# A gated linear recurrence with a SoLU feed-forward on one core: the constants' load moves behind the first inputs, and every step gets a new place in a written order

## The chip, the cores and the metric

The kernel runs on one core of a Trainium2 chip. The metric is device time in microseconds (us): the median over several executions of the whole program. A profile of one execution, with the times of all instructions, semaphores and DMA packets, stands beside the times.

## The reference

All arrays are float32. There are 4 batches, 8 heads, 768 positions, head dimension 48; the feed-forward has width 1024 over 3072 tokens of 384. The weights come as float64 and are converted on the chip.

```python
mag = np.sqrt(a_re * a_re + a_im * a_im)
scale = np.minimum(mag, 0.999) / (mag + 1e-06)
a_re_n, a_im_n = (a_re * scale, a_im * scale)
for t in range(S):                       # S_re, S_im start at zero, (B, H, D, D)
    ar, ai = (a_re_n[:, :, t, :, None], a_im_n[:, :, t, :, None])
    new_re = ar * S_re - ai * S_im
    new_im = ar * S_im + ai * S_re
    kv = np.einsum('bhd,bhe->bhde', k[:, :, t], v[:, :, t])
    S_re, S_im = (new_re + kv, new_im)
    y[:, :, t] = np.einsum('bhd,bhde->bhe', q[:, :, t], S_re)
# y is laid out as (B*S, H*D) = x, then:
h = x @ w_in
e = np.exp(h - np.max(h, axis=-1, keepdims=True))
solu = h * e / (np.sum(e, axis=-1, keepdims=True) + 1e-09)
ln = (solu - mean(solu)) / np.sqrt(var(solu) + 1e-06) * g_ln
out = ln @ w_out
```

## The kernel before

The 3072 tokens are cut into 24 chunks of 128 (6 stretches of time by 4 batches); two neighbouring chunks make a group, so there are 12 groups. The recurrence is done chunk by chunk in closed form: the logarithm of the gate's size and its angle are summed along time with matmuls against a triangle, q and k are scaled and turned by them, and then a chunk is causal attention plus a carried state of 96 by 48 per head. Behind it the same chunk goes through the feed-forward.

The work is written as small named steps, `name:number`, with a group's number or a chunk's. Those that matter here:

- Loads of a group, each one DMA on SP's queue: `load_ar`, `load_ai`, `load_q`, `load_k`, `load_v` (384 KB), `load_vr` (four DMAs of 48 KB). Group 0's a_re and a_im come in two halves of 192 KB, `load_ara`, `load_arb`, `load_aia`, `load_aib` (line 706), one for each chunk.
- Preparation of a group: `inverse` (two ACT passes, lines 824 and 825), `ratio` (two DVE passes, 830 and 831), `sure`, `tangent`, `square`, `secant`, `fourth`, `size` (852), `eps`, `lnm` (859), then the matmuls `total0`, `total1` (f_L), their exponentials `grow` and `decay`, `trig` (a table load on ACT, line 986), `angle` (922), `on` (927), from group 3 on a split in a high and a low part, `xh` (864) and `xl` (871), the matmuls `phase0`, `phase1`, and `nearest`, `part`, `sin`, `cos`, `exp` (the table load back, 989). `qs` and `ks` scale q and k. Group 0 does `inverse` to `lnm` and `angle`, `sin`, `cos` in halves, with an a or b at the end of the name.
- A chunk's attention: `q2`, `k2` and `kqb` (a block transpose on DVE, 1009) with `kqt0` (four DMAs), or for chunks 0 and 1 `qt`, `kt` (transposes on PE, 1021) with `qT`, `kT` (copies on ACT, 1027); `score0`, `score1` (1054), `mask0` (1059), `values` (1087), `carry`, `add`.
- A chunk's feed-forward: `turned_x` (1121), `up0`, `up1` (1128), `exp0`, `solu0` (1140), `spread`, `blocks` (1158) with `away` (four DMAs), or `zt` with `zT`; `down0`, `down1` (1193), `scale`, `store`.
- The weights, in seven pieces: `fetch` (DMA), `raised` (ACT, 752), `convert` (three DVE passes, 758 to 762); then `mean`, `meansum`, `centre` fold the mean and g_ln into w_out. `again` and `inspect` read each piece a second time for a check of its range; `judge` to `flag` make one word of all checks, which decides at the end whether a slower general path runs.

Each engine works through its instructions in the order in which the steps stand in one written string, `ORDER`; a step waits only for its own operands and buffers. A place in `ORDER` is therefore a place in five queues at once. The constants `f_mats` (identity, triangle and others, 320 KB, line 1280) are the only input that is loaded from ACT's queue, and stand ahead of all steps:

```python
    to_exp()
    nc.scalar.dma_start(out=mats, in_=nc.inline_tensor(fast_constants(), ...)...)
    ...
    for s in ORDER.split():
        nm, i = s.split(":")
        go(nm, int(i))
```

Two PSUM buffers (`ps_t`) serve `total`, `phase`, `qt`, `kt` and `zt` in turn; `f_bits`, which `raised` writes, has one buffer and shares it with `blocks`.

Of the kernel before, what the change touches and what calls it, by code (L numbers as in the profile page):

```python
# [516 lines left out]
init:0 load_aia:0 load_ara:0 inversea:0 load_arb:0 ratioa:0 load_aib:0 surea:0 load_q:0 tangenta:0 fetch:5 fetch:1  # L517
inverseb:0 squarea:0 ratiob:0 secanta:0 sureb:0 sizea:0 load_v:0 tangentb:0 epsa:0 load_k:0 lnma:0 squareb:0 secantb:0
fourthb:0 sizeb:0 total0:0 epsb:0 fourtha:0 raised:5 lnmb:0 decay0:0 grow0:0 total1:0 grow1:0 decay1:0 fetch:0 trig:0
anglea:0 convert:5 phase0:0 last:0 raised:1 qs0:0 angleb:0 convert:1 phase1:0 nearest0:0 part0:0 turn_ends:0  # L520
nearest1:0 ks0:0 ks1:0 sina:0 cosa:0 load_ai:1 qs1:0 part1:0 q2:0 tot:0 sinb:0 k2:0 cosb:0 exp:0 qt1:0 load_ar:1 qT1:0
raised:0 q2:1 kt1:0 k2:1 convert:0 kT1:0 inverse:1 ratio:1 kt0:0 qt0:0 qT0:0 kT0:0 fetch:2 score1:0 fetch:6 qt0:1
qT0:1 load_vr:0 score0:0 qt1:1 sure:1 raised:2 load_q:1 mask0:0 values:0 tangent:1 kt1:1 fetch:3 square:1 secant:1
turned_x:0 convert:2 qT1:1 up0:0 fetch:4 raised:6 size:1 eps:1 convert:6 lnm:1 fourth:1 onward:0 up1:0 gain:0 total1:1
load_k:1 kT1:1 raised:3 exp0:0 grow1:1 total0:1 decay0:1 grow0:1 carry:1 convert:3 solu0:0 decay1:1 trig:1 angle:1
kt0:1 phase1:1 ks1:1 qs0:1 kT0:1 add:1 phase0:1 ks0:1 score1:1 raised:4 nearest0:1 score0:1 nearest1:1 convert:4
part0:1 carry:0 part1:1 mean:0 mean:3 mean:7 add:0 sin:1 cos:1 mask0:1 load_q:2 q2:2 k2:2 mean:1 zt0:0 exp:1 load_ar:2
mean:4 mean:2 inverse:2 values:1 mean:5 kqb:2 turned_x:1 load_ai:2 ratio:2 mean:6 zT0:0 meansum:0 again:5 last:1
centre:3 centre:7 up1:1 sure:2 tangent:2 load_v:1 kqt0:2 square:2 zt1:0 centre:1 centre:2 secant:2 centre:0 centre:4
size:2 centre:6 eps:2 centre:5 up0:1 k2:3 turn_ends:1 qs1:1 score1:2 lnm:2 onward:1 centred:0 load_vr:1 score0:2 tot:1  # L530
down0:0 total0:2 zT1:0 total1:2 load_k:2 q2:3 exp0:1 fourth:2 mask0:2 down1:0 solu0:1 decay0:2 grow0:2 grow1:2
load_ar:3 decay1:2 kqb:3 trig:2 mixed:1 zt0:1 kqt0:3 last:2 values:2 angle:2 spread:0 zT0:1 on:2 phase1:2 ks1:2 norm:0
qs0:2 turned_x:2 phase0:2 carry:2 load_ai:3 nearest1:2 nearest0:2 up0:2 part1:2 part0:2 sin:2 add:2 cos:2 ks0:2 k2:4
q2:4 centred:1 exp:2 zt1:1 zT1:1 inverse:3 scale:0 up1:2 kqb:4 score1:3 score0:3 down0:1 mask0:3 ratio:3 exp0:2
turn_ends:2 spread:1 sure:3 solu0:2 load_q:3 values:3 tangent:3 load_v:2 down1:1 square:3 tot:2 turned_x:3 secant:3
size:3 load_k:3 carry:3 qs1:2 up0:3 kqt0:4 eps:3 norm:1 up1:3 k2:5 onward:2 zt1:2 lnm:3 lh:3 zt0:2 exp0:3 q2:5 scale:1
zT0:2 zT1:2 fourth:3 score1:4 ll:3 score0:4 mixed:0 total0:3 load_vr:2 total1:3 down0:2 kqb:5 down1:2 solu0:3 decay0:3
grow0:3 grow1:3 decay1:3 mask0:4 add:3 centred:2 trig:3 blocks:3 values:4 angle:3 on:3 xh:3 kqt0:5 store:1 store:0
spread:2 xl:3 last:3 phase1:3 turned_x:4 phase0:3 ks0:3 ks1:3 qs0:3 nearest0:3 score1:5 load_ar:4 centred:3 score0:5
nearest1:3 carry:4 load_ai:4 norm:2 part0:3 up0:4 part1:3 sin:3 cos:3 up1:4 mask0:5 turn_ends:3 exp:3 add:4 scale:2  # L540
k2:6 q2:6 away:3 inverse:4 values:5 exp0:4 kqb:6 ratio:4 down0:3 load_q:4 solu0:4 spread:3 turned_x:5 sure:4 load_v:3
tangent:4 qs1:3 down1:3 carry:5 kqt0:6 square:4 blocks:4 secant:4 size:4 onward:3 up0:5 away:4 eps:4 k2:7 norm:3 up1:5
q2:7 lnm:4 lh:4 tot:3 fourth:4 score1:6 ll:4 score0:6 exp0:5 total0:4 load_vr:3 load_k:4 kqb:7 total1:4 kqt0:7 solu0:5
scale:3 decay0:4 grow0:4 grow1:4 decay1:4 mask0:6 add:5 down0:4 trig:4 down1:4 centred:5 values:6 angle:4 on:4 xh:4
centred:4 qs0:4 xl:4 spread:4 last:4 store:2 phase1:4 turned_x:6 phase0:4 ks1:4 nearest0:4 ks0:4 nearest1:4 blocks:5
score1:7 carry:6 load_ai:5 part0:4 load_ar:5 part1:4 norm:4 score0:7 up0:6 sin:4 add:6 turn_ends:4 cos:4 exp:4 scale:4
away:5 store:3 inverse:5 mask0:7 up1:6 k2:8 q2:8 kqb:8 values:7 spread:5 exp0:6 ratio:5 down0:5 sure:5 load_q:5
solu0:6 turned_x:7 load_v:4 tangent:5 down1:5 square:5 qs1:4 kqt0:8 blocks:6 secant:5 onward:4 carry:7 up0:7 norm:5
size:5 eps:5 q2:9 k2:9 away:6 load_vr:4 lnm:5 up1:7 load_k:5 lh:5 fourth:5 scale:5 exp0:7 score1:8 ll:5 score0:8
total0:5 tot:4 kqb:9 total1:5 down0:6 kqt0:9 solu0:7 grow1:5 decay1:5 mask0:8 decay0:5 grow0:5 trig:5 down1:6 add:7  # L550
centred:7 blocks:7 values:8 angle:5 on:5 inspect:5 xh:5 centred:6 xl:5 spread:6 phase1:5 last:5 qs0:5 store:4
turned_x:8 phase0:5 ks1:5 load_ar:6 nearest1:5 nearest0:5 ks0:5 carry:8 load_ai:6 score0:9 score1:9 part1:5 part0:5
mask0:9 up1:8 sin:5 norm:6 up0:8 cos:5 add:8 turn_ends:5 scale:6 exp:5 inverse:6 store:5 k2:10 q2:10 values:9 kqb:10
ratio:6 exp0:8 solu0:8 away:7 turned_x:9 onward:5 down0:7 load_q:6 sure:6 down1:7 load_v:5 spread:7 tangent:6 square:6
blocks:8 qs1:5 kqt0:10 carry:9 secant:6 fourth:6 up0:9 norm:7 size:6 k2:11 away:8 eps:6 lnm:6 tot:5 load_vr:5 up1:9
q2:11 lh:6 scale:7 exp0:9 load_k:6 score0:10 score1:10 ll:6 total0:6 kqb:11 total1:6 down0:8 kqt0:11 solu0:9 grow1:6
decay1:6 mask0:10 decay0:6 grow0:6 trig:6 down1:8 add:9 centred:9 blocks:9 angle:6 values:10 on:6 xh:6 centred:8
store:6 xl:6 qs0:6 spread:8 last:6 phase1:6 turned_x:10 phase0:6 nearest0:6 ks1:6 nearest1:6 score1:11 carry:10
load_ai:7 score0:11 ks0:6 load_ar:7 away:9 part0:6 part1:6 cos:6 up0:10 sin:6 norm:8 mask0:11 up1:10 turn_ends:6
scale:8 exp:6 add:10 inverse:7 spread:9 store:7 values:11 k2:12 q2:12 kqb:12 ratio:7 exp0:10 down0:9 onward:6 solu0:10  # L560
load_q:7 turned_x:11 sure:7 down1:9 tangent:7 qs1:6 carry:11 load_v:6 kqt0:12 square:7 blocks:10 up0:11 secant:7
size:7 norm:9 eps:7 k2:13 away:10 load_vr:6 scale:9 lnm:7 tot:6 up1:11 q2:13 lh:7 fourth:7 exp0:11 score1:12 load_k:7
ll:7 score0:12 total0:7 kqb:13 total1:7 down0:10 centred:10 kqt0:13 solu0:11 grow1:7 decay1:7 mask0:12 decay0:7
grow0:7 trig:7 down1:10 add:11 blocks:11 angle:7 values:12 on:7 xh:7 last:7 store:8 spread:10 centred:11 qs0:7 xl:7
ks0:7 phase1:7 turned_x:12 phase0:7 nearest1:7 ks1:7 nearest0:7 score0:13 score1:13 part1:7 part0:7 mask0:13 sin:7
load_ar:8 away:11 carry:12 load_ai:8 up0:12 cos:7 add:12 norm:10 turn_ends:7 scale:10 exp:7 store:9 up1:12 k2:14 q2:14
inverse:8 values:13 kqb:14 ratio:8 exp0:12 solu0:12 down0:11 load_q:8 turned_x:13 sure:8 down1:11 load_v:7 tangent:8
carry:13 qs1:7 spread:11 kqt0:14 square:8 blocks:12 secant:8 norm:11 size:8 onward:7 k2:15 tot:7 eps:8 away:12 lnm:8
load_vr:7 fourth:8 up0:13 lh:8 load_k:8 up1:13 q2:15 score1:14 score0:14 ll:8 scale:11 total0:8 kqb:15 total1:8
exp0:13 decay0:8 grow0:8 centred:12 mask0:14 grow1:8 decay1:8 down0:12 kqt0:15 solu0:13 trig:8 down1:12 add:13  # L570
centred:13 blocks:13 angle:8 values:14 on:8 xh:8 store:10 spread:12 xl:8 last:8 phase1:8 turned_x:14 phase0:8 ks0:8
score0:15 qs0:8 nearest0:8 score1:15 ks1:8 nearest1:8 part0:8 carry:14 load_ai:9 part1:8 sin:8 norm:12 mask0:15 cos:8
add:14 load_ar:9 up1:14 turn_ends:8 exp:8 up0:14 away:13 k2:16 q2:16 scale:12 inverse:9 store:11 values:15 kqb:16
ratio:9 exp0:14 spread:13 load_v:8 solu0:14 turned_x:15 sure:9 down0:13 load_q:9 down1:13 tangent:9 blocks:14 square:9
# [38 lines left out]
def whole(ctx, tc, flag, q, k, v, a_re, a_im, moe_w_in, moe_w_out, moe_g_ln, out):  # L613
# [663 lines left out]


    to_exp()
    nc.scalar.dma_start(out=mats, in_=nc.inline_tensor(fast_constants(), name="f_mats_np").ap().rearrange("p (n t) -> p n t", n=5))  # L1280
    nc.vector.memset(unit, 1.0)
    nc.vector.memset(quarter, -0.5 * math.pi)
    nc.vector.memset(small, math.log(1e-6))
# [90 lines left out]
```

## Time and profile before

| | before |
|---|---|
| median of 3 runs | 415.65 us (415.19 to 415.83) |
| profiled execution: time | 415.1 us |
| profiled execution: span, first to last instruction | 413.1 us |
| PE / DVE / ACT / POOL busy | 379.1 / 337.0 / 299.0 / 64.5 us |
| mean granted TensorE clock | 0.996 |
| bytes moved by DMA | 74.17 MB, mean 180 GB/s |
| first matmul | 13.27 us |

Times in the text are counted from the span's start. The time of an execution is 2.0 us over its span. PE is TensorE's matmuls, DVE VectorE, ACT ScalarE, POOL GpSimd, SP the engine that issues nearly all DMAs; PEq, SPq and so on are the engines' queues. In a timeline's row stand the start, the time taken, the engine, the source line, the operation, what it writes and reads, how many were merged (x), and in brackets the idle time of the engine before it and what ended that.

### The profile page before, as it was taken

Reading aid. Unit: us, or ns where it says so; the run is one execution under the profiler, and the core shown is the slowest. Engines: PE = TensorE matmul, PEld = TensorE weight load, DVE = VectorE, ACT = ScalarE, POOL = GpSimd, SP = SyncE. Lnnn points to the kernel's source line nnn. Section 1 sums busy time; section 2 is a strip of 40 time slices with the busy share of each in tenths; the row PEclk is TensorE's granted clock in tenths of the full one; section 3 lists DMA queues with packets and bytes.
Section 4 is the critical chain, followed back from the end, with each engine's and each line's share of the span. In section 5 each row is a group of like instructions: output and inputs, shape, how many; then the busy total and the mean of one; then the engine's idle time right before and its main releaser. Section 6 shows DMA issues by size and latency. Waiting matters only on the chain.

```text
span 413.1 us, 15874 instructions
## 1 busy us (share of the span) xinstructions
PE 379.1 (92%) x6968; PEld 202.7 (49%) x6968; DVE 337.0 (82%) x414; ACT 299.0 (72%) x487; POOL 64.5 (16%) x140
## 2 busy tenths in 40 slices
PE   0368779999999999999999999999999999999995
PEld 0025334455645554654554554555645656546543
DVE  3798999779799899898899889988988988855530
ACT  4997977977887777887877976877976967721332
POOL 3000000112112112112122112112112122101111
PEclk9999999999999999999999999999999999999998
DMA  9995947695877778877787877967759768797551
GB/s 216 286 280 153 222 101 171 159 211 128 207 165 170 167 177 180 182 157 167 179 175 165 207 163 160 206 157 172 163 138 215 158 155 206 232 208 187 171 216 49
DMA packets 167741, 74.17 MB, mean 180 GB/s; under 512 B 142576, under 2 KB 156016, under 8 KB 166896
## 3 DMA queue, kind: packets, MB, share of 16 engines
q1 hardware_dynamic: 167376, 72.64, 74.7%
q8 instruction: 57, 0.93, 0.9%
q10 hardware_dynamic: 288, 0.43, 0.4%
q14 instruction: 20, 0.16, 0.1%
HBM read 38.87 MB, written 4.72 MB: 106 GB/s over the span
## 4 chain that ended last, share of the span: by engine, by line
PE 81%; ACT 8%; DVE 5%; DMA 2%; issue 1%; SPq 1%; DVEq 0%; ACTq 0%
PE f_h L1128 28%; PE f_o L1193 27%; PE f_y L1087 9%; PE f_score L1054 7%; PE f_d L1095 3%; PE f_L L876 2%; PE f_phase L876 2%; DMA f_q<-in_q_dram 1%; DMA f_ar<-in_a_re_dram 1%; ACT f_cs L951 1%; PE f_y L1203 1%; PE f_o L1203 1%; ACT L986 1%; ACT L989 1%; DVE f_kb L1009 1%
## 5 line engine op out<-in xcount | busy, mean ns | idle before, releaser
L1128 PE MATMUL f_h<-f_w_in,f_xT 128*32 128x512 f32 x1152 | 131.4, 593 | 1.4 <-ACT f_xT L1121 1.2
L1193 PE MATMUL f_o<-f_w_mix,f_zT 128*32 128x384 f32 x1280 | 108.6, 487 | 0.0
L1128 PEld LDWEIGHTS f_h<-f_w_in,f_xT 128*32 128x32 f32 x1152 | 40.9, 110 | 66.4 <-issue 64.3
L1193 PEld LDWEIGHTS f_o<-f_w_mix,f_zT 128*32 128x32 f32 x1280 | 42.8, 110 | 54.1 <-issue 51.5
L1009 DVE STREAM_TRANSPOSE f_kb<-f_kq 128x1536 f32<-128x1536 f32 x22 | 56.5, 2570 | 1.4 <-DMA f_kqT<-f_kb 0.7
L1140 DVE SCALAR_TENSOR_TENSOR f_z<-f_h,f_z 128x1024 f32<-128x1024 f32 x24 | 29.1, 1213 | 13.5 <-ACT f_z L1136 13.5
L1180 POOL TENSOR_SCALAR f_s<-f_s,f_sum 128x1 f32<-128x1 f32 x24 | 11.7, 485 | 182.1 <-ACT f_z L1174 181.9
L1136 ACT ACTIVATE f_z<-f_h 128x1024 f32<-128x1024 f32 x24 | 24.4, 1018 | 21.0 <-PE f_h L1128 21.0
L1087 PE MATMUL f_y<-f_att,f_v 128*16 128x128 f32 (+1 forms) x384 | 36.7, 273 | 0.8 <-DVE f_att L1059 0.8
L1054 PEld LDWEIGHTS f_score<-f_kqT 96*32 96x32 f32 x1536 | 32.5, 112 | 10.0 <-issue 10.0
L1087 PE MATMUL f_y<-f_att,f_vr 128*32 128x128 f32 x384 | 36.8, 273 | 0.0
L1059 DVE TENSOR_TENSOR f_att<-f_score,f_mats 128x1024 f32<-128x1024 f32 x24 | 29.3, 1220 | 8.5 <-PE f_score L1054 8.4
L1054 PE MATMUL f_score<-f_kqT 96*32 96x64 f32 (+3 forms) x1536 | 34.0, 238 | 0.0
L1087 PE MATMUL f_y<-f_kqT,f_state 96*32 96x128 f32 (+1 forms) x640 | 33.2, 272 | 0.0
L1174 ACT ACTIVATE f_z<-f_z,f_less 128x1024 f32<-128x1024 f32 x24 | 27.3, 1138 | 0.0
L869 POOL TENSOR_TENSOR f_ll<-f_lr,f_lh 128x768 fp32r<-128x768 f32 x9 | 16.6, 1849 | 65.6 <-ACT f_lh L864 57.9
L1087 PEld LDWEIGHTS f_y<-f_att,f_v 128*32 128x32 f32 (+1 forms) x384 | 22.0, 103 | 7.5 <-issue 6.4
L1158 DVE STREAM_TRANSPOSE f_zb<-f_z 128x1024 f32<-128x1024 f32 x20 | 24.8, 1238 | 0.0
L1000 DVE TENSOR_TENSOR f_kq<-f_cs,f_k 128x768 f32<-128x768 f32 x24 | 22.9, 955 | 2.1 <-ACT f_cs L951 1.2
L1000 DVE TENSOR_TENSOR f_kq<-f_cs,f_q 128x768 f32<-128x768 f32 x24 | 22.9, 953 | 1.1 <-PE f_d L1095 0.5
L1087 PEld LDWEIGHTS f_y<-f_att,f_vr 128*32 128x32 f32 x384 | 22.3, 109 | 1.7 <-issue 1.7
L1171 POOL TENSOR_SCALAR f_less<-f_sum 128x1 f32<-128x1 f32 x24 | 6.3, 266 | 88.7 <-DVE f_z L1140 88.7
(124 smaller groups left out, 643.9 us busy)
## 6 DMA issues: line engine op xcount, KB each, us to landing
f_kqT<-f_kb SPq DMA_DIRECT2D x88, 192.0 KB, 3.3
f_zT<-f_zb SPq DMA_DIRECT2D x80, 128.0 KB, 3.1
f_raw<-in_moe_w_out_dram SPq DMA_DIRECT2D x14, 384.0 KB, 5.0
f_raw<-in_moe_w_in_dram SPq DMA_DIRECT2D x5, 1024.0 KB, 6.7
f_q<-in_q_dram SPq DMA_DIRECT2D x12, 384.0 KB, 4.9
f_v<-in_v_dram SPq DMA_DIRECT2D x12, 384.0 KB, 5.2
f_k<-in_k_dram SPq DMA_DIRECT2D x12, 384.0 KB, 3.9
out_dram<-f_ot SPq DMA_DIRECT2D x23, 192.0 KB, 3.6
```

Of the source, the lines that this page charges most:

```text
L869: nc.gpsimd.tensor_tensor(out=t, in0=st[src], in1=st[hi].bitcast(FP), op=OP.subtract)
L1000: nc.vector.tensor_tensor(out=t, in0=T["cs", g][:, i * H:(i + 1) * H], in1=heads(T[nm, g][:, i]).unsqueeze(2).to_broadcast([P, H, 2, D]), ...
L1009: nc.vector.transpose(out=t, in_=T["kq", c].rearrange("p n h (f j) -> p j (n h) f", j=3))
L1054: nc.tensor.matmul(out=scores[r0:r0 + 32, x, r:], lhsT=QK[:, r // 32, x], rhs=QK[:, r // 32:, H + x], start=True, stop=True)
L1059: nc.vector.tensor_tensor(out=st["att"].rearrange("p (i u) t -> p i u t", u=2), in0=scores.rearrange("p (i u) t -> p i u t", u=2), in1=mat ...
L1087: nc.tensor.matmul(**product)
L1128: nc.tensor.matmul(out=st["h"][r:r + 32, half * 512:(half + 1) * 512], lhsT=st["xT"][:, c * P + r:c * P + r + 32], rhs=w_in[:, c, half * 5 ...
L1136: nc.scalar.activation(out=z, in_=h, func=AF.Exp, accum_out=sums[:, n:n + 1])
L1140: nc.vector.scalar_tensor_tensor(out=st["z"], in0=st["h"], scalar=1.0, in1=st["z"], op0=OP.mult, op1=OP.mult, accum_out=st["sum"][:, 0:1])
L1158: nc.vector.transpose(out=st["zb"], in_=st["z"].rearrange("p (c s f) -> p s c f", s=4, f=32))
L1174: nc.scalar.activation(out=st["z"], in_=st["z"], func=AF.Square, bias=st["less"], accum_out=st["sum"][:, 1:2])
L1193: nc.tensor.matmul(out=st["o"][rows], lhsT=zT, rhs=w[:, c], start=(c == 0), stop=(c == KF - 1))
```

## The change

The load of `f_mats` leaves ACT's queue and becomes a step, `constants:0`, on SP's queue. It stands behind the four halves of a_re and a_im and the two DMAs of `fetch:5`. Of group 0's halves a_re's now comes before a_im's. The string `ORDER` is written anew from end to end; no step but `constants:0` is added or left out, and no instruction's shape changes. The diff, cut to its core (the ORDER lines around the start, group 9's middle and the end):

```diff
-init:0 load_aia:0 load_ara:0 inversea:0 load_arb:0 ratioa:0 load_aib:0 surea:0 load_q:0 tangenta:0 fetch:5 fetch:1
-inverseb:0 squarea:0 ratiob:0 secanta:0 sureb:0 sizea:0 load_v:0 tangentb:0 epsa:0 load_k:0 lnma:0 squareb:0 secantb:0
-fourthb:0 sizeb:0 total0:0 epsb:0 fourtha:0 raised:5 lnmb:0 decay0:0 grow0:0 total1:0 grow1:0 decay1:0 fetch:0 trig:0
-anglea:0 convert:5 phase0:0 last:0 raised:1 qs0:0 angleb:0 convert:1 phase1:0 nearest0:0 part0:0 turn_ends:0
-nearest1:0 ks0:0 ks1:0 sina:0 cosa:0 load_ai:1 qs1:0 part1:0 q2:0 tot:0 sinb:0 k2:0 cosb:0 exp:0 qt1:0 load_ar:1 qT1:0
-raised:0 q2:1 kt1:0 k2:1 convert:0 kT1:0 inverse:1 ratio:1 kt0:0 qt0:0 qT0:0 kT0:0 fetch:2 score1:0 fetch:6 qt0:1
-qT0:1 load_vr:0 score0:0 qt1:1 sure:1 raised:2 load_q:1 mask0:0 values:0 tangent:1 kt1:1 fetch:3 square:1 secant:1
-turned_x:0 convert:2 qT1:1 up0:0 fetch:4 raised:6 size:1 eps:1 convert:6 lnm:1 fourth:1 onward:0 up1:0 gain:0 total1:1
...
-mask0:16 decay0:9 grow0:9 centred:14 trig:9 down1:14 add:15 store:12 kqt0:17 solu0:15 qs1:9 blocks:15 angle:9
-values:16 on:9 xh:9 spread:14 xl:9 centred:15 phase0:9 turned_x:16 phase1:9 last:9 ks0:9 score1:17 nearest0:9 ks1:9
...
-down1:22 zt0:23 zt1:23 judges:0 inspect:2 inspect:6 scale:22 zT0:23 judgew:0 centred:23 zT1:23 store:20 count:0 flag:0
-spread:23 down0:23 down1:23 norm:23 store:22 scale:23 store:23 down2:23 scale2:23 store2:23
+init:0 load_ara:0 load_aia:0 load_arb:0 inversea:0 load_aib:0 ratioa:0 surea:0 fetch:5 tangenta:0 inverseb:0
+constants:0 load_q:0 ratiob:0 squarea:0 secanta:0 sureb:0 tangentb:0 fetch:1 fourtha:0 squareb:0 secantb:0 load_k:0
+sizea:0 fetch:0 epsa:0 sizeb:0 epsb:0 fourthb:0 lnma:0 load_vr:0 load_ar:1 lnmb:0 total0:0 raised:5 convert:5
+load_ai:1 grow0:0 total1:0 decay0:0 decay1:0 load_v:0 grow1:0 trig:0 qs0:0 angleb:0 raised:1 qs1:0 phase1:0 anglea:0
+phase0:0 nearest1:0 convert:1 fetch:2 nearest0:0 part1:0 raised:0 ks1:0 cosb:0 ks0:0 part0:0 last:0 sina:0 cosa:0
+sinb:0 fetch:6 convert:0 q2:0 qt0:0 k2:0 exp:0 qt1:0 inverse:1 qT0:0 k2:1 qT1:0 gain:0 kt1:0 ratio:1 kt0:0 kT1:0
+sure:1 load_k:1 kt1:1 score1:0 q2:1 kT0:0 fetch:3 score0:0 tangent:1 square:1 mask0:0 qt1:1 raised:2 secant:1 kT1:1
+convert:2 qT1:1 values:0 qt0:1 turned_x:0 turn_ends:0 raised:6 up1:0 load_q:1 size:1 up0:0 eps:1 fetch:4 convert:6
+tot:0 lnm:1 qT0:1 fourth:1 total0:1 raised:3 total1:1 exp0:0 grow0:1 convert:3 decay0:1 decay1:1 solu0:0 grow1:1
...
+tangent:2 square:2 centre:4 turn_ends:1 centre:5 score0:2 score1:2 secant:2 centre:6 centre:0 size:2 load_vr:1
+centred:0 exp0:1 centre:7 eps:2 k2:3 q2:3 lnm:2 spread:0 tot:1 down0:0 total1:2 solu0:1 fourth:2 onward:1 total0:2
+mask0:2 grow0:2 kqb:3 load_q:2 grow1:2 decay0:2 decay1:2 trig:2 angle:2 down1:0 mixed:1 kqt0:3 norm:0 zt0:1 ks0:2 on:2
...
+trig:9 ks1:9 angle:9 on:9 ks0:9 kqt0:17 store:12 blocks:15 xh:9 spread:14 values:16 xl:9 store:13 qs0:9 last:9
...
+blocks:22 again:2 away:22 inspect:6 inspect:2 centred:22 spread:22 up0:23 again:3 scale:21 inspect:3 up1:23 exp0:23
+down0:22 down1:22 solu0:23 store:20 again:0 inspect:0 judges:0 judgew:0 norm:22 zt0:23 scale:22 centred:23 zT0:23
+zt1:23 zT1:23 count:0 down0:23 spread:23 norm:23 flag:0 down1:23 store:22 scale:23 down2:23 scale2:23 store:23
+store:21 store2:23
...
     to_exp()
-    nc.scalar.dma_start(out=mats, in_=nc.inline_tensor(fast_constants(), name="f_mats_np").ap().rearrange("p (n t) -> p n t", n=5))
     nc.vector.memset(unit, 1.0)
...
-    steps["gain", 0] = gain
+    def constants():
+        nc.sync.dma_start(out=mats, in_=nc.inline_tensor(fast_constants(), name="f_mats_np").ap().rearrange("p (n t) -> p n t", n=5))
+
+    steps["gain", 0], steps["constants", 0] = gain, constants
```

## Prediction

> **What bounds the kernel now.** First the page's slices, to see which engine is full and when:
>
> ```profile
> PE   0368779999999999999999999999999999999995
> DVE  3798999779799899898899889988988988855530
> ACT  4997977977887777887877976877976967721332
> PEclk9999999999999999999999999999999999999998
> ```
>
> PE is full from the seventh slice (60 us) to the last; ahead of that DVE and ACT carry more than PE. The busy time by stretch says it in us (columns: PE, PEld, DVE, ACT, POOL):
>
> ```profile
> 5.58:16.08 10.50, 1.50 (x8) 0.20 (x8) 5.41 (x10) 8.81 (x21) 0.00 (x0) 1.00 0.99 273
> 16.08:60.00 43.92, 30.61 (x451) 15.83 (x451) 40.80 (x53) 39.44 (x64) 0.90 (x2) 1.00 0.81 205
> 60.00:77.00 17.00, 16.78 (x248) 7.40 (x248) 16.79 (x23) 12.43 (x22) 0.28 (x1) 1.00 0.70 156
> 77.00:100.00 23.00, 22.76 (x428) 11.27 (x424) 18.04 (x20) 17.65 (x30) 5.39 (x10) 1.00 0.85 180
> 100.00:396.00 296.00, 295.84 (x5661) 161.07 (x5653) 250.53 (x291) 213.64 (x343) 52.01 (x109) 1.00 0.77 179
> ```
>
> PE idles 0.16 us between 100 and 396, but 28 us ahead of 100 (100 less 1.50, 30.61, 16.78 and 22.76). Its work is unchanged, so only the start can give time. From 16 to 60 us DVE idles 3.1 us and ACT 4.5: there a step comes earlier only if its chain does. The waits of PE between 13 and 100 us name the chains:
>
> ```profile
> PE f_L L881 <- DVE f_lr L859: 14.7, 2, 13.3
> PE f_phase L881 <- ACT f_x L922: 4.7, 2, 2.8
> PE f_turned L1021 <- DVE f_kq L1000: 2.6, 1, 2.6
> PE f_mean L783 <- ACT f_meanp L781: 1.8, 1, 1.8
> ```
>
> The first is the 13.3 us until the first matmul. It begins in the timeline with the loads:
>
> ```profile
> 0.72 0.45 SPq L706 DMA_DIRECT2D f_ai<-in_a_im_dram  x1
> 0.75 0.39 ACTq L1280 DMA_DIRECT2D f_mats<-f_mats_np  x1
> 1.23 2.38 SPq L706 DMA_DIRECT2D f_ar<-in_a_re_dram  x2
> 5.58 0.52 ACT L824 ACTIVATE f_lr<-f_ar 128x384 f32<-128x384 f32 x1 [3.58 <-DMA f_ar<-in_a_re_dram]
> ```
>
> ACT is ready at 2.0 and waits 3.58 us for half of a_re, which is second behind a_im and beside the constants.
>
> **1. The first load.** By the packet records the constants' first packet goes at 1.78, 1.03 us behind its issue, and a_im's only at 2.65, 1.93 behind its own: the constants hold it for 0.9. A load into an idle queue later (f_ar at 69.03) has its first packet at 70.06, also 1.03. The four halves land at 4.65, 5.56, 6.44 and 7.32, 0.88 apart. In the new order a_re's half is alone and first: 1.75 for the first packet, 0.9 for its 1024 packets, and 0.85 from last packet to landing (3.85 to 4.65 and 4.61 to 5.56 for the first two) makes 3.5, against 5.56: 2.05 us earlier. Bounds: 0.9 (the swap alone, if the late packet isn't the constants' doing) and 2.25 (no ramp). a_im's half at 4.4 is in time for `ratioa` at 4.6. The Trainium skill ("DMA: Bandwidth & Descriptors", Issuing engines are not separate DMA queues) says that DMAs of all issuing engines share the same 16 DMA engines, and a second issuer saves only sequencer time; by it the change of queue brings nothing and only the place in the order counts, the 0.9 with it.
>
> **2. The constants.** SP issues them seventh. Behind the halves (6.1) come 768 KB of `fetch:5` (2.4 us before, from 9.18 to 11.56) and 320 KB (1.0 at the same rate): 9.5. f_L needs them at 13.1. Cost nothing; they would have to slip by 3.6. q (1.86 us from 7.32 to 9.18) lands at 11.4, first needed at 16.7; the w_in piece of `fetch:1` at 15.0 as before, needed at 17.7. All later loads only move by places in a stream that carries the same bytes.
>
> **3. Group 0 to the trig load.** The first ACT, DVE chain moves by 2.05 as it is: `sure` at 5.9 instead of 7.87. Then the new order puts both `size` and both `lnm` together, and half b's last `lnm` ends at 14.2 (16.16 before), half a's at 13.1 (13.2). f_L takes 1.50 for eight matmuls, so the second one ends at 16.1 (17.7), and behind four exponentials ACT loads the trig table at 17.0 instead of 18.68: 1.7 gained.
>
> **4. To the first mask.** Between the two table loads ACT has 7.1 us of passes, now with `raised:0` (1.15) in them, and waits 1.0 for the second f_phase; the load back starts at 26.5 instead of 26.73, with 1.15 us of work less behind it. DVE has `convert:0` done at 26.2 (32.06). But `inverse:1` (1.7) now stands before the copies that free the two PSUM buffers, so PE's transposes wait: `qT` at 29.5, `kt` of chunk 0 at 30.1 to 32.0, `kt1:1` to 33.0, scores to 35.4 cold or 34.4 warm. The rate is the open point:
>
> ```profile
> 13.27 1.50 PE L881 MATMUL f_L<-f_lr,f_mats 128*32 128x384 f32 x8 [13.27 <-DVE f_lr L859]
> 44.55 1.50 PE L881 MATMUL f_L<-f_lr,f_mats 128*32 128x384 f32 x16
> ```
>
> Eight matmuls took what sixteen take later, though PEclk reads 1.00; the scores at 33.44 still took 1.24 for 32, the transposes at 34.61 0.64 for four (1.09 before). PE there had run with one gap of 0.4 since 28.66. `mask0:0` thus starts at 34.4 to 35.4, against 34.77, but `tangent:1` is done before it, and DVE goes straight to `convert:2`: its end is 38.8 to 39.7 against 40.09. The skill ("TensorE: Matmul & The Clock Gate", Part 1) has half rate until a window of about 3.4 us is busy; counted from 30.1 that puts the change at 33.5, which is the warm case, 1.3 gained here.
>
> **5. To 60 us.** From there ACT and DVE have the same work as before without a gap: `raised:6`, `eps:1`, `lnm:1`, exponentials, table, `convert:4`, table, `kqb:2`. `up` of chunk 0 needs `turned_x:0`, which now stands ahead of less on ACT: 38.0 instead of 39.13. The copy of f_parts stood behind `turned_x:1` and now before it, so f_mean comes at 58.2 to 59.0 instead of 59.90.
>
> **6. 60 to 100 us.** Two new waits of PE: `lnm:2` now stands behind `k2:3` and `q2:3` (0.96 each), so f_L of group 2 waits 0.7 behind `down0:0`; `on:2` stands behind `kqb:3` and waits for `angle:2`, so f_phase waits 0.7. Against them the gaps before f_mean, f_phase (0.2) and f_d (0.2) shrink. I carry the lead through: `down0:2`, 101.5 before, starts 0.7 to 1.8 earlier. I take 1.3, between the cold and the warm case.
>
> **7. The full stretch.** PE's steps stand in nearly the same order in each group. One path has little slack: table, `angle`, `on`, `xh`, `xl`, f_phase.
>
> ```profile
> 225.22 1.23 DVE L1158 STREAM_TRANSPOSE f_zb<-f_z 128x1024 f32<-128x1024 f32 x1
> 226.38 0.90 DVE L927 SCALAR_TENSOR_TENSOR f_x<-f_on,f_x 1x768 f32<-1x768 f32 x1
> 227.21 0.54 DVE L904 TENSOR_TENSOR f_q<-f_q,f_ar 128x384 f32<-128x384 f32 x1
> 228.25 0.96 DVE L871 SCALAR_TENSOR_TENSOR f_xl<-f_x,f_xh 128x768 fp32r<-128x768 f32 x1 [0.50 <-ACT f_xh L864]
> ```
>
> Between `on` and `xl` DVE has 1.04 us. The new order moves `blocks` (1.16 to the next start) from before `on` into that place, and in groups 4, 7 and 9 a `ks` (0.47) with it: `xl` comes 0.12 later, or 0.59. From the end of `xl` to the matmul that reads it groups 3 to 10 have 0.37, 0.82, 0.48, 0.41, 0.46, 0.73, 0.17 and 0.27 us; so group 7 loses 0.13 and group 9 0.42. Cost 0.55, from nothing (the path may lead by more, as `add` now stands earlier) to 2.5 with no slack anywhere (six times 0.12 and three times 0.59). I take 0.3. `load_q` and `load_v` come half a group later and land some 5 us before their use: nothing.
>
> **8. The end.** `again:0` (1 MB) comes last, behind `again:3`; at the 7.9 us that 2.2 MB took from 390.88 its `inspect` ends some 1.9 us before the count that PE waits for. `store:21` goes to the very end of SP's queue, 0.34 us between the last half store and the flag; the end waits for ACT's store, issued later (408.45). Cost nothing, at most 0.3.
>
> **Sum.** 1.3 less 0.3: 1.0 us. The profiled time 415.1 becomes 414.1; it stands 0.55 under the median of 415.65, so I forecast 414.6 for the median. What a measurement of this kernel can tell from no change is about 0.2%, 0.8 us.
>
> **Rivals.** (a) The lead is used up on the way. For it: the table load back moves only 0.25, and the first mask may come later than before; against it: DVE's `convert:0` and `tangent:1` are ahead of their old places. A lead of 0.7 at 100 us less 0.55 leaves 415.5, the same. (b) The late packet is not the constants' doing; the halves then land 0.9 earlier only, the lead of 1.3 falls by 1.1, and the tight path takes the rest: 415.75. For it: only one load is seen behind the constants; against it: the two rows of 1.03. (c) Slower: `blocks` ahead of `xl` holds f_phase in all nine groups, 2.5 us in all. It decides as soon as it passes the start's lead; with 1.3 that is 416.85, with 0.7 417.4. For it: slack of 0.17 to 0.82 that a later `angle` eats; against it: with the slacks as they are only two groups are short.
>
> **How the numbers follow.** Forecast 0.45, (a) 0.2, (b) 0.1, (c) 0.25: more than its slacks alone would give, as every group passes there and each lost 0.3 us counts nine times. Faster is the forecast's; same is (a) and (b). The range goes from 413.2 (1.8 at 100 us, the tight path free, 0.6 for PE's gaps) to 416.9, (c) with the lead of 1.3.
>
> **What would show it.** Right: ACT's first pass at 3.5, trig load at 17.0, load back at 26.5, `convert:2` done by 39.7, `down0:2` 1.3 earlier, `xl` directly behind `blocks`, PE idle from 100 to 396 under 0.6 us. Wrong: a first pass at 4.6 (b), f_mean not before 59.9 (a), waits of f_phase on `xl` of over 0.2 in most groups (c).

## The result, and the profile after

The changed kernel takes 419.95 us (median of 4 runs, 418.08 to 421.07) against 415.42 for the kernel before beside it: a ratio of 1.0089, 95% interval 1.0062 to 1.0116. The forecast was 414.6 (413.2 to 416.9), so its sign was wrong. The profiled execution took 418.08 us with a span of 416.2, the shortest of the four: its trace accounts for 3.0 of the 4.5 us between the medians, and the rest is seen in times only.

The slices of the changed kernel:

```profile
PE   0448789999999999999999999999999999999993
DVE  4798999787989998889989989989989998764440
ACT  6988978877877877967967967877876966722330
PEclk9999999999999999999999999999999999999998
```

PE waits more in the third slice (4 for 6), where it waits 5.5 us for DVE's f_kq, and is fuller in the second and sixth; its last slice is emptier (3 for 5). The stretches, with the columns PE, PEld, DVE, ACT, POOL:

```profile
16.08:60.00 43.92, 30.13 (x460) 16.03 (x464) 41.62 (x53) 38.55 (x62) 0.91 (x2) 1.00 0.81 204
100.00:396.00 296.00, 294.19 (x5602) 158.14 (x5598) 252.50 (x287) 212.32 (x341) 61.81 (x111) 1.00 0.78 177
```

PE idles 1.8 us between 100 and 396 instead of 0.16, DVE is busy 2.0 us more for nearly the same instructions, and POOL 9.8 us more. The waits of PE:

```profile
PE f_phase L877 <- DVE f_xl L872: 1.4, 4, 0.6
PE f_mean L784 <- ACT f_meanp L782: 1.1, 1, 1.1
PE f_o L1194 <- DMA f_zT<-f_zb: 0.3, 1, 0.3
```

The first row is new: four of the nine groups wait for f_xl. It shows less than it costs. The four matmuls of f_phase for one chunk take 0.89 us to the next step when nothing is late; in groups 4, 6, 9 and 10 they took 1.45, 1.44, 1.39 and 1.77, together 2.5 us more, while the row counts 1.4. The second matmul normally starts 0.28 us behind the first, inside its 0.44 us; idle time counts only from the first one's end, and the one after a wait again needs 0.28 instead of 0.18. So each of these waits costs 0.26 or 0.27 us more than the row counts for it.

To see where time is won and lost I took the same amount of PE work (by its matmuls) in both traces and compared the times at which it was reached. The changed kernel leads by 1.9 us at 93 us and by 2.0 at 130, by 0.7 to 1.4 from 220 to 285, by about 0.5 at 310, and is 0.5 behind at 323 and 1.8 behind at 361. At the last matmul it is 1.53 behind (409.12 against 407.59). Behind that the last issue of a store comes 0.87 later in both, and from it to the end of the span it takes 6.24 us instead of 4.61: the end costs another 1.6.

### The profile page after: what moved, and what is told of

It reads as the page before. It is cut to its first block, busy times and chain, and to the rows that moved or that the text cites. A ratio compares the mean times of both kernels' runs of the same rounds, so it can differ in the third digit from the quotient of the medians.

```text
span 416.2 us, 15890 instructions
## 1 busy us (share of the span) xinstructions
PE 379.3 (91%) x6968; PEld 201.0 (48%) x6968; DVE 342.4 (82%) x414; ACT 298.3 (72%) x487; POOL 73.5 (18%) x140
## 4 chain that ended last, share of the span: by engine, by line
PE 45%; DVE 21%; ACT 17%; issue 7%; DMA 5%; SPq 2%; POOL 0%; DVEq 0%; ACTq 0%
PE f_o L1194 15%; PE f_h L1129 13%; PE f_y L1088 4%; PE f_score L1055 4%; DVE f_kb L1010 3%; DMA f_zT<-f_zb 3%; DVE f_z L1141 2%; DVE f_kq L1001 2%; DMA f_kqT<-f_kb 2%; DVE f_ai L831 2%; PE f_phase L877 2%; ACT L990 2%; DVE f_att L1060 2%; ACT f_u L846 2%; SPq L1164 2%
## 5 line engine op out<-in xcount | busy, mean ns | idle before, releaser
L1129 PEld LDWEIGHTS f_h<-f_w_in,f_xT 128*32 128x32 f32 x1152 | 39.3, 110 | 64.4 <-issue 64.1
L1010 DVE STREAM_TRANSPOSE f_kb<-f_kq 128x1536 f32<-128x1536 f32 x22 | 54.7, 2488 | 0.9 <-DMA f_kqT<-f_kb 0.5
L1172 POOL TENSOR_SCALAR f_less<-f_sum 128x1 f32<-128x1 f32 x24 | 12.6, 525 | 153.8 <-DVE f_z L1141 153.7
L1137 ACT ACTIVATE f_z<-f_h 128x1024 f32<-128x1024 f32 x24 | 24.4, 1018 | 19.2 <-PE f_h L1129 19.2
L1088 PE MATMUL f_y<-f_att,f_v 128*32 128x128 f32 (+1 forms) x384 | 36.8, 273 | 0.8 <-DVE f_att L1060 0.8
L1181 POOL TENSOR_SCALAR f_s<-f_s,f_sum 128x1 f32<-128x1 f32 x24 | 14.9, 619 | 121.9 <-ACT f_z L1175 100.2
L1055 PEld LDWEIGHTS f_score<-f_kqT 96*32 96x32 f32 x1536 | 31.3, 110 | 9.5 <-issue 7.9
L1055 PE MATMUL f_score<-f_kqT 96*32 96x96 f32 (+3 forms) x1536 | 33.6, 235 | 0.2 <-DMA f_kqT<-f_kb 0.2
```

Of the source, the lines that this page charges most:

```text
L1010: nc.vector.transpose(out=t, in_=T["kq", c].rearrange("p n h (f j) -> p j (n h) f", j=3))
L1055: nc.tensor.matmul(out=scores[r0:r0 + 32, x, r:], lhsT=QK[:, r // 32, x], rhs=QK[:, r // 32:, H + x], start=True, stop=True)
L1088: nc.tensor.matmul(**product)
L1129: nc.tensor.matmul(out=st["h"][r:r + 32, half * 512:(half + 1) * 512], lhsT=st["xT"][:, c * P + r:c * P + r + 32], rhs=w_in[:, c, half * 5 ...
L1137: nc.scalar.activation(out=z, in_=h, func=AF.Exp, accum_out=sums[:, n:n + 1])
```

## The experiments

Each ratio is to the kernel before, timed beside the run on the same chip (the first row is the result above; e1 to e8 ran on one chip, e9 to e14 on another). The third column is the ratio less 1, times 416 us. Its interval is some 0.6 to 1.5 us to either side, and the difference between two rows carries the intervals of both.

| run | ratio, 95% interval | us against before |
|---|---|---|
| changed kernel | 1.0089, 1.0062 to 1.0116 | +3.7 |
| e1_loads | 0.9938, 0.9915 to 0.9961 | -2.6 |
| e2_start | 0.9944, 0.9924 to 0.9963 | -2.3 |
| e3_rest | 1.0156, 1.0121 to 1.0190 | +6.5 |
| e4_store | 1.0067, 1.0044 to 1.0090 | +2.8 |
| e5_blocks | 1.0172, 1.0141 to 1.0204 | +7.2 |
| e6_scales | 1.0077, 1.0042 to 1.0111 | +3.2 |
| e7_add | 1.0019, 1.0001 to 1.0036 | +0.8 |
| e8_before_add | 1.0036, 1.0020 to 1.0051 | +1.5 |
| e9_are_first | 0.9975, 0.9959 to 0.9992 | -1.0 |
| e10_constants | 0.9973, 0.9957 to 0.9989 | -1.1 |
| e11_add_end | 0.9976, 0.9962 to 0.9990 | -1.0 |
| e12_start_oldloads | 0.9995, 0.9979 to 1.0011 | -0.2 |
| e13_store_last | 1.0024, 1.0005 to 1.0044 | +1.0 |
| e14_three | 1.0039, 1.0017 to 1.0060 | +1.6 |

### Which half of the change does what

**The loads alone** (e1_loads), in the old order:

```diff
-init:0 load_aia:0 load_ara:0 ... surea:0 load_q:0 tangenta:0 fetch:5 fetch:1
+init:0 load_ara:0 load_aia:0 ... surea:0 tangenta:0 fetch:5 constants:0 load_q:0 fetch:1
```

> The kernel before with the loads alone changed: a_re's half ahead of a_im's, the constants behind the first weight piece; every other step in its old place. Theory A (the loads carry the start): ACT's first pass at 3.5 us instead of 5.6, the trig table load 1.5 to 2 us earlier than 18.7, and of that 1 to 2 us are still there at 100 us, as the old order passes them on: a time of 413.4 to 414.4 against 415.4. Theory B (the loads only let it, the new places of ACT's and DVE's steps carry it): the first pass moves by 2 us, but the old order stands behind later loads and the second table load, so under 0.5 us are left at 100 us: 415.0 to 415.6.

Measured: 413.75 us, 2.6 faster than before. ACT's first pass is at 3.45, the trig load at 16.93. Theory A: three moves in the queue of loads bring the whole gain, and the old order passes it on. The profiled execution took 415.5 us, so its trace says nothing of the size.

**The new start, the old rest** (e2_start):

```diff
-ORDER = the new string
+ORDER = the new string up to down0:3, then all that is left of the old string in its order
```

> The new order up to the first half of the last matmul of chunk 3 (some 112 us), the old order behind it. Theory A (PE's lead of 2.0 us at 110 us is real time, and what eats it is the order of the later groups and of the end): the lead stays, PE idles under 0.5 us from 110 us on, the end is as before: 413.4. Theory B (the lead can't be kept, since DVE and ACT do not come earlier by as much, and the slack of 0.2 to 0.8 us ahead of f_phase turns into waits with any order): f_phase waits for f_xl in most groups and the time is within 0.8 us of 415.4.

Measured: 413.62 us, 2.3 faster than before, as e1. One row of the stretches says that the lead can be kept:

```profile
100.00:396.00 296.00, 296.00 (x5642) 162.56 (x5645) 247.60 (x288) 213.90 (x344) 52.04 (x108) 1.00 0.78 182
```

PE idles for nothing in 296 us, DVE is busy 247.6 us instead of 252.5 and POOL 52.0 instead of 61.8: theory A. What loses the lead is the new order behind 112 us. This is also, with e1, the fastest version of all: both beat both kernels.

**The old start, the new rest** (e3_rest):

```diff
-ORDER = the old string
+ORDER = the old string up to down0:3, then all that is left of the new string but constants:0
```

> The converse of the first hybrid: loads and order of before up to the first half of the last matmul of chunk 3, the new order behind it. Theory A (the new order of the later groups loses time by itself: 3.8 us of PE's time on the way and 1.6 at the end): with no lead to spend the loss shows whole, some 418.5 to 421 against 416.0. Theory B (the waits in the later groups are only PE's lead catching up with DVE and ACT): without the lead they do not appear, and only the end's 1.6 us are left: 417 to 417.8.

Measured: 422.65 us, 6.5 slower, more than theory A asked for. The waits are there without any lead to catch up: theory B falls. New start (-2.3) and new rest (+6.5) add up to +4.2, near the +3.7 of both.

**The square of the start** (e12_start_oldloads):

```diff
-ORDER = the old string; constants on ACT's queue
+ORDER = the new string with load_aia:0 first, up to down0:3, then the old one; constants on ACT's queue
```

> The new order up to the first half of the last matmul of chunk 3 and the old one behind it, as in the run of the new start, but with the loads of before: the constants on ACT's queue ahead of all steps and a_im's half first. With it the two edits of the start stand in a square: old loads and old order 415.9, new loads and old order 413.75, both new 413.6. Theory A (the loads carry the gain and the new places in the start add nothing): within 0.5 us of 415.9, or slower. Theory B (the new places make a gain of their own, which the loads only replace): 414 to 415.

Measured: 415.67, ratio 0.9995. Theory A: the new places of the start alone bring nothing that can be measured; the trig load is at 18.81 and the load back at 28.03, later than before (18.68 and 26.73).

**The two edits of the loads** (e9_are_first, e10_constants), each alone in the kernel before:

```diff
-init:0 load_aia:0 load_ara:0 inversea:0        (e9: the swap)
+init:0 load_ara:0 load_aia:0 inversea:0
-tangenta:0 fetch:5 fetch:1                      (e10: the constants)
+tangenta:0 fetch:5 constants:0 fetch:1
```

> The kernel before with one swap: a_re's half is loaded ahead of a_im's; the constants stay on ACT's queue ahead of all. Theory A (the constants in flight hold the first packet for 0.9 us): a_re's half lands where a_im's did, at 4.65, ACT's first pass starts at 4.6 instead of 5.6; of these 0.95 us some 0.4 are left at 100 us (the two edits together move the first pass by 2.05 and left 0.9): 415.5 against 415.9. Theory B (the order of the halves is all, the late packet is not the constants' doing): the pass starts at 3.5 and the time is that of the loads alone, 413.8.

> The kernel before with the constants alone moved to SP's queue behind the first weight piece; a_im's half stays ahead of a_re's. Theory A: a_im's first packet goes at 1.75 instead of 2.65, all halves land 0.9 to 1.1 earlier, the first pass starts at 4.5 and the time is about 415.4. Theory B: a_im's first packet stays at 2.65, the pass at 5.6, the time at 415.9.

The timeline of e9, and then of e10, at ACT's first pass:

```profile
4.66 0.52 ACT L824 ACTIVATE f_lr<-f_ar 128x384 f32<-128x384 f32 x1 [2.65 <-DMA f_ar<-in_a_re_dram]
```

```profile
4.74 0.52 ACT L825 ACTIVATE f_lr<-f_ar 128x384 f32<-128x384 f32 x1 [2.74 <-DMA f_ar<-in_a_re_dram]
```

5.58 before, 4.66 and 4.74 with one edit, 3.51 with both: each is worth 0.9, and the constants in flight did hold the first packet: in e10, where they leave later, a_im's first packet goes at 1.83 instead of 2.65. In time the two are worth 1.0 and 1.1 us, together 2.1 of e1's 2.6, which the intervals allow. That is more than I expected of each (0.4 and 0.5): I had gone by e1's trace.

### What loses time in the middle

**blocks back** (e5_blocks), the step that the prediction named, in groups 4 to 11 (here group 10):

```diff
-on:10 kqt0:19 blocks:17 xh:10
+blocks:17 on:10 kqt0:19 xh:10
```

> The changed kernel with one step per group moved: blocks (DVE's transpose of 1.23 us) back from between on and xl to ahead of on, in groups 4 to 11. Theory A (as predicted: blocks between on and xl makes f_xl late): the four waits of f_phase on f_xl go and the time falls by some 2.5 us from the changed kernel's. Theory B (it is the scalings of q and k ahead of on, 0.47 us each, that make xl late, and blocks fills the 0.9 us in which DVE would wait for ACT's xh anyway): on, xh and xl come 0.5 to 1.1 us later still, f_phase waits for f_xl in more groups and longer, and the time rises by 2 to 6 us.

Measured: 422.81 us, 3.5 slower than the changed kernel. The waits of PE in e5:

```profile
PE f_phase L877 <- DVE f_xl L872: 2.2, 4, 0.6
PE f_phase L877 <- ACT f_xh L865: 2.0, 3, 1.2
```

Theory A falls: ahead of on the transpose makes f_phase wait more often and longer. Its place between on and xl, beside ACT's xh, is not what makes f_xl late.

**The scalings behind xl** (e6_scales), groups 3 to 10 (here group 10):

```diff
-trig:10 ks1:10 ks0:10 angle:10 qs1:10 on:10 ... xl:10 store:15
+trig:10 angle:10 on:10 ... xl:10 ks1:10 ks0:10 qs1:10 store:15
```

> The changed kernel with the scalings ks and qs that stand between trig and xl moved to directly behind xl, in groups 3 to 10; blocks stays between on and xl. Theory A (blocks makes f_xl late): xl comes earlier by 0.5 to 1.4 us all the same, since DVE has less ahead of it, but the waits are due to blocks and shrink only by part: under 1 us gained. Theory B (the scalings do): the four waits of f_phase on f_xl go, and with them 2.5 us: some 417.4 against the changed kernel's 419.9. If instead the time stays, the waits only move to a consumer of the scaled q and k (the block transposes and the scores).

Measured: all four waits of f_phase are gone, but the time is 418.86, 0.5 us under the changed kernel by the ratios and inside the intervals. Others have taken their place:

```profile
PE f_L L877 <- POOL f_ll L870: 1.7, 2, 1.2
PE f_o L1194 <- ACT f_ot L1221: 1.1, 1, 1.1
```

So 0.5 to 1.4 us less ahead of xl frees f_phase, but DVE is as busy as in the changed kernel (252.7 us from 100 to 396), and another consumer is late next. Neither theory names the cause; inconclusive by its time.

**add behind kqb** (e7_add). Why is DVE busy longer with the same work? The changed kernel's timeline in group 6, DVE and POOL, and PE at f_phase:

```profile
187.87 0.55 DVE L1105 TENSOR_TENSOR f_state<-f_d,f_state 96x384 f32<-96x384 f32 x1
188.04 1.84 POOL L870 TENSOR_TENSOR f_ll<-f_lr,f_lh 128x768 fp32r<-128x768 f32 x1 [5.16 <-ACT f_lh L865]
188.45 1.83 DVE L1106 TENSOR_TENSOR f_state<-f_state,f_tot 96x384 f32<-96x384 f32 x1
197.77 0.90 DVE L872 SCALAR_TENSOR_TENSOR f_xl<-f_x,f_xh 128x768 fp32r<-128x768 f32 x1
198.73 0.45 PE L877 MATMUL f_phase<-f_xl,f_mats 128*128 128x384 f32 x1 [0.28 <-DVE f_xl L872]
```

The second operation of `add`, 0.55 us everywhere in the kernel before, takes 1.83: it starts 0.41 behind POOL's `ll` and ends 0.40 behind ll's end, as if it had stood until then. In the kernel before, kqb's transpose runs beside ll, and add comes 3.4 us after ll's end:

```profile
189.37 2.57 DVE L1009 STREAM_TRANSPOSE f_kb<-f_kq 128x1536 f32<-128x1536 f32 x1
189.42 1.85 POOL L869 TENSOR_TENSOR f_ll<-f_lr,f_lh 128x768 fp32r<-128x768 f32 x1 [4.68 <-ACT f_lh L864]
194.69 0.55 DVE L1105 TENSOR_TENSOR f_state<-f_state,f_tot 96x384 f32<-96x384 f32 x1
```

In the changed kernel add is held so in groups 4, 6, 9, 10 and 11 (1.83 to 2.08); the first four are those whose f_phase waits.

```diff
-tot:3 add:5 fourth:4 ll:4 ... kqb:7 down0:4        (group 4; so too in 5, 6, 9, 10, 11)
+tot:3 fourth:4 ll:4 ... kqb:7 add:5 down0:4
```

> The changed kernel with the add of the group's odd chunk moved from ahead of kqb to directly behind it, in groups 4, 5, 6, 9, 10 and 11. Theory C (new: the second operation of add, 0.55 us with two inputs in SBUF, starts while POOL's subtraction ll runs, and then takes 1.83 to 2.08 us, as in the five groups 4, 6, 9, 10 and 11 of the changed kernel; this 1.3 us is what makes xl late): every add takes 0.55, the f_phase waits of groups 4, 6, 9 and 10 go, the time falls by 2 to 2.5 us to some 417.5. Theory B (the scalings ahead of on make xl late): DVE has the same work ahead of xl, the waits of f_phase stay, the time stays within 0.5 us of 419.9.

Measured: 417.09 us, 2.9 under the changed kernel. Group 6 in e7:

```profile
187.79 1.85 POOL L870 TENSOR_TENSOR f_ll<-f_lr,f_lh 128x768 fp32r<-128x768 f32 x1 [5.16 <-ACT f_lh L865]
190.66 0.55 DVE L1106 TENSOR_TENSOR f_state<-f_state,f_tot 96x384 f32<-96x384 f32 x1
196.44 0.91 DVE L872 SCALAR_TENSOR_TENSOR f_xl<-f_x,f_xh 128x768 fp32r<-128x768 f32 x1
```

Every add takes 0.55, xl starts 8.65 us behind ll instead of 9.73, no f_phase waits for xl, and the stretch reads

```profile
100.00:396.00 296.00, 295.73 (x5630) 163.32 (x5626) 247.24 (x288) 213.86 (x345) 60.12 (x111) 1.00 0.79 181
```

with DVE busy 247.2 us instead of 252.5. Theory C. It also says what e6 lacked: there f_phase was free too, but add's second operation still took 1.84 to 2.05 us in the same five groups, and only 0.5 us were gained.

**The converse in the kernel before** (e8_before_add), groups 4 to 11:

```diff
-load_k:4 kqb:7 ... mask0:6 add:5        (group 4)
+load_k:4 add:5 kqb:7 ... mask0:6
```

> The converse, in the kernel before: the add of the group's odd chunk moved to ahead of kqb (in groups 10 and 11 to behind ll), where POOL's ll runs; loads and all else as before. Theory C: the second operation of add takes 1.8 to 2.1 us in most of groups 4 to 11, DVE's kqb comes some 2.4 us later, and the slack of 0.2 to 0.8 us ahead of f_phase is used up in part: 1 to 3 us slower than before, 417 to 419. Theory B (add beside ll costs nothing): within 0.5 us of 416.0, every add at 0.55.

Measured: 417.75 us, 1.5 slower. Group 6 of e8:

```profile
189.17 1.84 POOL L869 TENSOR_TENSOR f_ll<-f_lr,f_lh 128x768 fp32r<-128x768 f32 x1 [4.69 <-ACT f_lh L864]
189.58 1.84 DVE L1105 TENSOR_TENSOR f_state<-f_state,f_tot 96x384 f32<-96x384 f32 x1
199.88 0.44 PE L876 MATMUL f_phase<-f_xl,f_mats 128*128 128x384 f32 x1 [0.21 <-DVE f_xl L871]
```

add's second operation fell beside ll in groups 6, 7, 8 and 9 only, and f_phase waits in exactly these four; in groups 4 and 5 it started 0.46 before ll and took 0.55, and f_phase does not wait. That is the cause of 2.9 of the lost microseconds, shown in both directions.

### The end

**store:21 back** (e4_store), and **store:21 last in the kernel before** (e13_store_last):

```diff
-up1:23 exp0:23 ... again:0 ... store:23 store:21 store2:23      (e4: the changed kernel)
+up1:23 exp0:23 store:21 ... again:0 ... store:23 store2:23
-exp0:23 store:21 ... store:23 down2:23 scale2:23 store2:23      (e13: the kernel before)
+exp0:23 ... store:23 down2:23 scale2:23 store:21 store2:23
```

> The changed kernel with store:21 alone moved from SP's last place to behind exp0:23, ahead of again:0. Theory A (this 192 KB store, issued at 409.22 us between the halves of the last one, delays the landing of the last stores and so the end): the stretch from the last issue to the end of the span falls from 6.2 to 4.6 us, as before, and the time by 1.6: 418.3 against 419.9. Theory B (the end waits only for ACT's own store, and the longer tail is chance): the stretch stays over 6 us and the time within 0.5 us of 419.9.

> The kernel before with store:21 alone moved to SP's last place, between the halves of the last store, as in the changed kernel. Theory A (the 192 KB store between the halves delays their last packets): the packets of SP's half store and store:21 end 1.7 to 2.6 us behind ACT's last issue instead of at it, the stretch from that issue to the end of the span grows from 4.4 to 4.7 us to 5.5 or more, and the time by about 1. Theory B (the longer tail of the changed kernel has another cause at the end): the stretch stays under 5 us, the time within 0.4 us of before's.

e4: 0.9 us under the changed kernel by the ratios, with overlapping intervals; the stretch from the last issue to the end is 5.56 us, not 4.6. e13: 1.0 slower than before, the stretch 5.61. The stores of e13 in the list of DMA issues (KB each, median us from issue to landing):

```profile
out_dram<-f_ot SPq DMA_DIRECT2D x1, 96.0 KB, 4.0
out_dram<-f_ot ACTq DMA_DIRECT2D x1, 96.0 KB, 3.6
```

In the kernel before the first of them reads

```profile
out_dram<-f_ot SPq DMA_DIRECT2D x1, 96.0 KB, 1.6
```

SP's half store, issued ahead of store:21, landed 1.6 us behind its issue in the kernel before, 3.5 in the changed one and takes 4.0 here. Over all profiles that have the landing, it is 3.5 to 4.3 in the six with store:21 behind it (the changed kernel, e3, e5, e6, e7, e13) and 1.6 to 1.9 in eight without; e4 is the exception, with 3.2 and nothing behind it on the queue. The store between the halves so costs 1.0 (0.2 to 1.8 by its interval). Moving it back in the changed kernel brought less, perhaps because it now stands ahead of again:0 on SP: that load leaves 0.5 us later, and the matmul of the count waits 0.7 for `inspect` (f_row), where it waited 0.3 for f_zT. About 0.9 us of the longer stretch stays in e4 (5.56) and e14 (5.55), where store:21 no longer stands between the halves, and in e14 SP's half store landed at 1.8 again; the cause is not found.

**Three edits together** (e14_three), and **add moved and the old order from chunk 17 on** (e11_add_end):

```diff
 e14: e7's and e4's moves, and
-load_vr:10 ... away:18
+away:18 load_vr:10
 e11: e7's moves, and
-ORDER = the string of e7
+ORDER = the string of e7 up to down1:17, then all that is left of the old string in its order
```

> The changed kernel with three edits: add behind kqb in six groups, store:21 ahead of again:0, and load_vr:10 (four DMAs, 2.64 us of SP's queue) from ahead of away:18 to behind it. Theory A (these three are what loses the time): e7's 417.1 less 0.9 for the store and 0.3 to 0.7 for away: 415.3 to 416, about before's time; the lead at 340 us is over 1 us and no matmul waits for f_zT. Theory B (the new order of the last groups loses by more than these): 416.5 or more.

> The changed kernel with add behind kqb (as in the run of that edit alone, 417.1) and, from behind the last matmul of chunk 17 on (some 327 us), the old order. Theory A (the waits at add and the end are what the new order costs, and nothing else of size): PE idles under 1 us from 100 to 400 us, the stretch from the last issue to the end falls to 4.6 us, and the time is within 0.5 us of the new start with the old rest, 413.3 to 414.3. Theory B (the new order loses more in the middle that the profile of one run does not show): over 415.

e14: 417.68, no better than add alone; theory B. The waits for f_xl are gone and that of f_o for f_zT is down to 0.2, but PE waits 0.6 for f_ot, 0.6 for f_row and 0.3 for a late v. e11: 414.87, 1.8 under e7 by the ratios, which were taken on two chips. Its trace has PE idle 0.5 us from 100 to 396 and a stretch of 5.03 at the end; the time lies between the two theories. The 1.3 us to e2 are only partly located: its f_L waits for ll in groups 9 and 11, with 0.15 and 0.7 us more than the 0.89 of an undisturbed group.

So, by ratios: new start -2.3; new order behind it +6.0, of which add beside ll 2.9, everything from chunk 17 on 1.8 (store:21 alone about 1.0), and the rest of the middle 1.3, not settled. The last two terms are differences between rows whose intervals nearly touch or overlap.

## Why the prediction was wrong, point by point

**1, the first load: right.** 3.51 for a predicted 3.5, and e9 and e10 show both parts. Rival (b), the late packet, is refuted. By the page that the prediction set beside it, the change of queue brings nothing and only the place in the order counts. Taking the constants out of the way alone moved ACT's first pass by 0.84 (e10), but that edit changed their queue and their place together, so no run here parts the two.

**2, the constants: right.** They landed at 10.02 (9.5), and f_L waited for f_lr, not for them.

**3 to 5, to 60 us: right, and a little low.** Trig load at 16.93 (17.0), load back at 26.13 (26.5), mask0:0 at 33.68 (34.4 to 35.4), convert:2 done at 38.12 (38.8 to 39.7), `up` of chunk 0 at 37.40 (38.0), f_mean at 57.57 (58.2 to 59.0). Rival (a) falls. PE's rate rose earlier than the prediction counted (33.5): the 64 scores at 32.08 took 1.51 us, where 32 had taken 1.24 to 1.30 in the kernel before. And e12 and e1 show that it was the loads: I had put part of the gain down to the new places of size, lnm and inverse, which by themselves bring nothing that can be measured (-0.2, interval -0.9 to 0.5).

**6, the lead at 100 us: mis-sized.** down0:2 at 99.57 instead of 101.54: 1.97 for my 1.3, over my bound of 1.8. Of the two new waits, f_phase's of 0.8 came as priced (0.7), f_L's did not.

**7, the tight path: this step failed.** I had the right path and the right place of the loss, and rival (c) even its size (2.5 us at f_phase), but the wrong cause and so the wrong likelihood; that the size agrees is luck, as (c) had it from nine groups and the trace has it from four. The sum put this step at 0.3 us; with add beside ll it cost 2.9, and the order behind the start 6.0 in all. It took every duration from rows in which the instruction ran beside its old neighbours. `add` was read as work that leaves the path ("the path may lead by more, as add now stands earlier"); I did not ask what POOL does at its new place. There add's second operation grew from 0.55 to 1.83 or more in five groups of nine. The tell that the prediction named, waits of over 0.2 on xl in most groups, came in four of nine. blocks, on which I hung the cost, is harmless: e7 leaves it between on and xl and no f_phase waits for xl, and moved ahead of on it makes things worse (e5).

**8, the end: failed too.** I set store:21 at nothing, at most 0.3 us, by its issue on SP's queue. At its new place it costs 1.0 us (e13): with its 192 KB behind it, the half store already in flight lands some 2 us later. The stretch behind the last issue grew by 1.6 in all, of which 0.9 stays without store:21 there and is open.

The mechanism is one that the Trainium skill states ("SBUF — State Buffer", Who interferes with whom): a DVE instruction with two inputs in SBUF contends with a GpSimd instruction that reads SBUF, and the one that starts first keeps the shared port to its end while the other stands. What this case shows agrees: add's second operation (both inputs in SBUF) started 0.17 to 0.41 us behind ll in the groups where it was late, and ended 0.4 behind ll's end. kqb's transpose (one input) and add's first operation (one input from PSUM) ran beside ll, having started 0.05 to 0.4 us ahead of it, and neither was held: add's first operation took its 0.55, the transpose 2.45 in e7 against 2.40 behind ll in the changed kernel, and ll 1.83 to 1.87 throughout. The other direction shows in POOL's small instructions, here beside DVE's line 840, which reads two inputs from SBUF, and beside mask0 (line 1060), which reads one from PSUM:

```profile
119.03 0.90 POOL L1172 TENSOR_SCALAR f_less<-f_sum 128x1 f32<-128x1 f32 x1
132.57 0.21 POOL L1172 TENSOR_SCALAR f_less<-f_sum 128x1 f32<-128x1 f32 x1 [3.90 <-DVE f_z L1141]
```

Most of POOL's 9.8 us more are its small instructions, which take longer in the mean (f_less 525 ns for 266). They are not what costs the time: e7 keeps them (POOL is busy 60.1 us from 100 to 396). What no run shows is an add that holds ll up: in e8 it ran on 0.1 us into ll, which took its 1.85.

## What to carry to other kernels

When a step moves to a new place, price it by what runs beside it there, on all engines: here a 0.55 us DVE instruction cost 1.3 us more wherever it started during POOL's 1.85 us pass, and DVE's busy time over the whole execution (342.4 us for the instructions that took 337.0 before, and 335.9 in e7) told of it. POOL's did not: it is 64.5 before, 73.5 in the changed kernel and still 71.8 in e7. A lead won at the start is kept only if the order behind it has room: try the two halves of such a change apart, since here the loads alone were 2.6 us faster and the rest of the change cost 6. A wait inside a pipelined run of matmuls can cost more than the idle row shows: 2.5 us for 1.4 here.

## What had not been expected of the hardware

With a 192 KB store issued 0.4 us behind it on the same queue, a 96 KB store landed 3.5 to 4.3 us behind its issue instead of 1.6 to 1.9 (but 3.2 in e4, without one).

The mean granted clock between 16 and 60 us reads 0.84 in the profiles of e2, e6, e7 and e11, against 1.00 in the changed kernel's own. That does not mean that the changed kernel's PE ran at full rate there: the eight transposes at 27 us took 1.91 us in it and 1.91 us in e7, where the reading from 19.2 to 31.6 is 0.50. The rates differ only in the next twelve, 2.49 us against 2.85. e2's lead at 93 us was 1.4 instead of 1.9; whether this is the clock's doing was not tried apart.
